# Transposes of 128 rows cut into two halves of 64 rows, a whole group per PSUM tile, in an attention and expert kernel

## The chip, the cores and the metric

The kernel runs on one core of one Trainium2 chip. The metric is the device time of one execution in microseconds. Three runs of the kernel before took 462.81, 463.68 and 463.78 us, the median is 463.68 us.

## The reference

Attention over 8 batches, 12 heads, 448 positions and a head size of 64, with q and k normalised row by row, is followed by a layer of 8 experts, of which each token takes one and each expert keeps 80 tokens at most. Tokens that no expert keeps give rows of zeros.

```python
q_n, k_n = rmsnorm(q, g_q), rmsnorm(k, g_k)          # x / sqrt(mean(x*x) + 1e-6) * g
attn = softmax(q_n @ k_n.transpose(0, 1, 3, 2) / sqrt(64))
x = (attn @ v).transpose(0, 2, 1, 3).reshape(3584, 768)
logits = x @ w_gate                                   # 3584 x 8
expert_idx, gate_w = argmax(logits), softmax(logits)[expert_idx]
for e in range(8):
    tok = the tokens of e, those 80 with the largest gate_w where there are more
    out[tok] = gate_w[tok] * (relu(x[tok] @ w1[e]) @ w2[e])   # 768 -> 1024 -> 768
```

## The kernel before

Four heads of one batch make a group; there are 24 groups, 3 to a batch. A row tile `qk` holds, on its 128 partitions, two heads `u` of 64 positions each, and along the free axis 14 blocks: 7 position classes `x` for each of two further heads `hh`. Every group goes through these steps: ScalarE squares q and k (line 253), VectorE sums (261), ScalarE and VectorE form the inverse root (`rstd`, 272 to 276), VectorE multiplies (`qn`, 289), TensorE turns q and k (`transp`, 301) and ScalarE copies the turned rows out of PSUM into `qkT` (314 with the gain, 316 without). Then come 7 steps `score` and `av`: four pairs of 64x64 matmuls make scores of 64 keys for 448 queries of four heads (326), ScalarE takes the exponential of 128x896 (329), and the product with v is added up in `po` over the 7 steps (341). The program has float32 score and product matmuls as two instructions each in the profile, so a step is 8 instructions on line 326 and 8 on line 341. VectorE adds the exponentials up over the steps (`presum`, 357 and 359), for the softmax's denominator. After step 7 ScalarE copies `po` to `us` (348), and `xout` turns `us` back to rows (606), copies them to `xb` (611) and sends them to a scratch array in DRAM with three DMAs of the SP queue (619, 620).

Per batch, `zl` (376) makes the gate's sums and the denominators of the 3 groups in one tile, by 48 matmuls of 64x32; `gate1` copies its two halves out (381, 385) and adds them on VectorE (388); `gate1t` turns the result (393); `gate1v`, `gate2`, ... and the pieces of `merge` (line 482 on, PSUM tiles named `mp`) pick each token's expert and keep the list of the best 80 per expert. After the last batch the lists are finished and the experts' products run (905, 924), while weights come in and rows are scattered by DMA.

The order is written out by hand. The main loop goes over slots of two steps. A slot's order is: `begin` work, the scores of two steps, `presum` of the two steps before, `mid` work, the products `av` of those two steps, `end` work. `at_slot` puts a piece of work into a slot and one of these places. On every engine instructions run in this order. PSUM is divided so: `tp_ps` has two buffers of one bank (512 float32), for the turned tiles `tp`, `xp`, `zt`; `sc_ps` has two buffers of two banks, for the scores `ps`, the gate's sums `zl` and the scratch `mp` of `merge`; `po_ps` has one buffer of two banks. An instruction that writes a buffer waits until the last reader of its former content is done.

In `transp(g, a, f)` the 7 turns of a tensor are cut into `f` = 0 with 4 and `f` = 1 with 3, each with a PSUM tile and a copy of its own, each in a slot of its own; in `xout(g, u)` the two halves `u` have 4 turns, a PSUM tile, a copy and a slot each. Each turn is one instruction:

```python
nc.tensor.transpose(tp[:, x * 128:(x + 1) * 128], qn[...128 rows x 128 columns...], ident[:, :])
```

It loads 128x128 float32 as weights and streams the identity of 128 columns past them.

Of the kernel before, what the change touches and what calls it, by code (L numbers as in the profile page):

```python
# [10 lines left out]
F32 = mybir.dt.float32  # L11
BF16 = mybir.dt.bfloat16
AF = mybir.ActivationFunctionType
# [4 lines left out]
PSUM = bass.MemoryType.PSUM  # L18
# [3 lines left out]
def kernel(  # L22
# [13 lines left out]
    nc = tc.nc  # L36

    B, H, S, D = q.shape
# [9 lines left out]
    NX = S // 64  # L48
# [4 lines left out]
    NJ = SM // 128  # L53
    NQ = H // 4
    NG = B * NQ
# [17 lines left out]
    ident = cpool.tile([128, 128], F32, name="ident")  # L73
# [15 lines left out]
    def gains():  # L89

        t = gk[0]
        grow = t[:1, 256:384]
        nc.vector.tensor_mul(grow, t[:1, 0:128], t[:1, 128:256])
        nc.vector.tensor_scalar_mul(grow, grow, 1.0 / math.sqrt(D))
        gp = tpps.tile([128, 512], F32, tag="tp", name="gp")
        nc.tensor.matmul(gp[:, 0:1], grow, one[:, :], start=True, stop=True)
        nc.vector.tensor_copy(gqk[:, :], gp[:, 0:1])

# [100 lines left out]
        load_weights(wpool, e, e)  # L199

    gpool = ctx.enter_context(tc.tile_pool(name="gate", bufs=2))
    tpps = ctx.enter_context(tc.tile_pool(name="tp_ps", bufs=2, space=PSUM))
    ctx.enter_context(tc.manual_schedule())

    ps_stack = ExitStack()
# [10 lines left out]
    with av_stack:  # L216
# [75 lines left out]
                    rs[:, lo:hi].rearrange("p (hh x) -> p hh x", x=NX)  # L292
                    .unsqueeze(3).to_broadcast([128, h1 - h0, NX, D]))

        def transp(g, a, f):

            tp = tpps.tile([128, 512], F32, tag="tp", name="tp")
            qn = st[g]["qn%d" % a]
            x0, n = (0, 4) if f == 0 else (4, NX - 4)
            for x in range(n):  # L300
                nc.tensor.transpose(  # L301
                    tp[:, x * 128:(x + 1) * 128],
                    qn[:, 2 * (x0 + x):2 * (x0 + x) + 2].rearrange("p h d -> p (h d)"),
                    ident[:, :])
            if f == 0:
                st[g]["T%d" % a] = qktpool.tile([128, 2, S], F32, tag=f"qkT{a}", name="qkT")
            o = st[g]["T%d" % a][:, :, x0 * 64:(x0 + n) * 64].rearrange(
                "q u (x p) -> q x u p", p=64)
            i = tp[:, :n * 128].rearrange("q (x u p) -> q x u p", u=2, p=64)

            if g == 0 and a and f == 0:
                nc.vector.tensor_scalar_mul(o, i, gqk[:, :])
            elif a == (g == 0):
                nc.scalar.activation(o, i, AF.Copy, scale=gqk[:, :])  # L314
            else:
                nc.scalar.copy(o, i)  # L316

        def score(r):
            g, x = divmod(r, RD)
# [41 lines left out]
        def zl(b, groups):  # L361


            if groups[0] == 0:
                gst[b]["zl"] = scps.tile([128, 2, 512], F32, tag="sc", name="zl")
            t = gst[b]["zl"]
            for i in groups:
                s = st[NQ * b + i]
                for c in range(4):
                    for r in range(2):  # L370
                        p = slice(64 * r, 64 * r + 64)
                        if c // 2 == r:
# [15 lines left out]
                nc.vector.tensor_add(zsb[:, c], zsb[:, c], other[:, c])  # L388

        def gate1t(b):  # L390
            zt = tpps.tile([128, 512], F32, tag="tp", name="zt")
# [204 lines left out]
            return [[row, lambda: vbeat((0, 1))], [experts, lambda: vbeat((2, 3)), vtied],  # L596
                    [own, vahead], [counts, vput], [place], [turn]]

        def xout(g, u):

            b, i = divmod(g, NQ)
            xp = tpps.tile([128, 512], F32, tag="tp", name="xp")
            us = st[g]["us"]
            for j in range(NJ + 1):
                c = j * 128 if j < NJ else S - 128
                nc.tensor.transpose(xp[:, j * 128:(j + 1) * 128], us[:, u, c:c + 128],  # L606
                                    ident[:, :])
            if u == 0:
                st[g]["xb"] = prep.tile([128, NJ + 1, 256], F32, tag="xb", name="xb")
            xb = st[g]["xb"]  # L610
            nc.scalar.copy(xb[:, :, u * 128:(u + 1) * 128],  # L611
                           xp[:, :].rearrange("p (j d) -> p j d", d=128))
            if u == 0:
                return
# [26 lines left out]
        def at_slot(where, s, f, *a):  # L641
            where.setdefault(s, []).append((f, a))
# [5 lines left out]
        lo, hi = HALF  # L648
        for f, *a in ((square, 0, lo), (square, 0, hi), (squares, 0, lo), (root, 0, lo),
                      (square, 1, lo), (squares, 0, hi), (root, 0, hi), (square, 1, hi),  # L650
                      (inverse, 0, lo), (normalise, 0, lo), (inverse, 0, hi),
                      (normalise, 0, hi), (squares, 1, lo), (root, 1, lo), (squares, 1, hi),
                      (root, 1, hi), (transp, 0, 0), (transp, 0, 1), (inverse, 1, lo),
                      (normalise, 1, lo), (inverse, 1, hi), (normalise, 1, hi), (gains, ),
                      (exptable, ), (transp, 1, 0)):
            at_slot(mid, -10, f, *([0] if a else []), *a)
        for g in range(NG):
            b0 = g * RD // 2
            odd = g % 2
            at_slot(begins, max(b0 - 11, -10), load_qk, g)  # L660
            at_slot(begins, b0 - 4, load_v, g)
            if g:
                for a in range(2):
                    at_slot(mid, b0 - 7 + a if g > 1 else -1, square, g, a)
                    at_slot(end, b0 - 7 + a if g > 1 else -1, squares, g, a)
                at_slot(mid, b0 - 5 if g > 1 else 0, rstd, g)
                for a in range(2):
                    at_slot(mid, b0 - 5 + a if g > 1 else 0, normalise, g, a)
            for a in range(2):
                for f in range(2):  # L670
                    t = b0 - 4 + 2 * a + f
                    if g == 0 and a + f < 2 or g == 0 and a > f:
                        continue
                    if g < 2:
                        t += 2 if g == 1 and a + f == 0 else 1
                    at_slot(end, t, transp, g, a, f)
            at_slot(end, b0 + 4 + odd, xout, g, 0)
            at_slot(end, b0 + 5 + odd, xout, g, 1)
        for b in range(B):
            b0 = (NQ * b + NQ - 1) * RD // 2  # L680
            if b == B - 1:
                at_slot(end, b0 + 3, zl, b, range(NQ - 1))
                at_slot(end, b0 + 4, zl, b, range(NQ - 1, NQ))
                at_slot(end, b0 + 4, gate1, b)
                at_slot(end, b0 + 5, gate1t, b)
# [67 lines left out]
    hot = tpps.tile([128, 512], F32, tag="tp", name="hot")  # L753

    def busy(n):

# [220 lines left out]
```

## Time and profile before

| | |
|---|---|
| median of 3 runs | 463.68 us (462.81 to 463.78) |
| profiled execution, its own time | 463.21 us |
| its span, first to last instruction | 461.3 us |
| TensorE busy | 440.2 us (95%) |
| VectorE busy | 358.3 us (78%) |
| ScalarE busy | 327.6 us (71%) |
| mean granted TensorE clock | 0.982 |

Between the span and the execution's own time lie 1.9 us. A share of busy time is a mean over the whole span; the attention part goes up to about 394 us, the experts' part takes the rest. PE stands for TensorE's matmuls, PEld for its weight loads, DVE for VectorE, ACT for ScalarE. A group of pipelined matmuls that overlap counts its time once.

### The profile page before, as it was taken

The numbers are of one execution on the slowest core, as the hardware profiler recorded it, in microseconds if no ns is written. First come the engines' busy times: TensorE is split into PE (matmuls) and PEld (weight loads), VectorE is DVE, ScalarE is ACT, GpSimd is POOL, SyncE is SP. The second block draws the span as 40 slices with busy tenths as digits, with TensorE's granted clock in tenths as the row PEclk, the third lists the DMA queues.
The fourth block names the chain that finished last, engine by engine and source line by source line (L and its number), as shares of the span: only waits on it lengthen the run. The fifth ranks groups of instructions, "written<-read, shape, count | busy, mean of one in ns | idle before, by whom it ended". The sixth has DMA issues, their size and how long they took to land.

```text
span 461.3 us, 11332 instructions
## 1 busy us (share of the span) xinstructions
PE 440.2 (95%) x4639; PEld 215.7 (47%) x4639; DVE 358.3 (78%) x650; ACT 327.6 (71%) x537; POOL 64.6 (14%) x126
## 2 busy tenths in 40 slices
PE   6999999999999999999999999999999999789894
PEld 5344444453444434443444444534444344348673
DVE  5788759995999878987998699959996877454451
ACT  6788878887888868986988699778887766301111
POOL 4010000200040004000510030001200010362311
PEclk9799999999999999999999999999999999979998
DMA  8999565898489966992799949956996376749991
GB/s 235 261 245 322 175 191 157 148 255 296 144 159 253 304 179 129 239 339 58 184 234 249 349 104 216 299 176 197 180 263 201 93 155 268 278 111 335 365 351 44
DMA packets 67530, 100.83 MB, mean 219 GB/s; under 512 B 7880, under 2 KB 59176, under 8 KB 66200
## 3 DMA queue, kind: packets, MB, share of 16 engines
q1 hardware_dynamic: 51184, 70.05, 47.0%
q0 software_dynamic: 16000, 29.61, 33.5%
q8 instruction: 36, 0.59, 0.5%
q10 hardware_dynamic: 296, 0.46, 0.3%
q14 instruction: 14, 0.11, 0.1%
HBM read 101.11 MB, written 39.89 MB: 306 GB/s over the span
## 4 chain that ended last, share of the span: by engine, by line
PE 84%; issue 7%; DVE 3%; ACT 3%; POOL 2%; DMA 1%; POOLq 0%
PE ps L326 30%; PE po L341 28%; PE tp L301 9%; PE xp L606 6%; PE zl L376 5%; POOL out_dram L937 2%; PE hot L758 1%; PE zt L393 1%; PE mp L496 1%; ACT zo L385 1%; DMA qk<-in_q_dram 1%; PE py L924 1%; POOL xg L868 1%; ACT zsb L381 1%; PE mp L550 1%
## 5 line engine op out<-in xcount | busy, mean ns | idle before, releaser
L329 ACT ACTIVATE at<-ps 128x896 f32<-128x896 f32 x168 | 146.4, 923 | 16.9 <-PE ps L326 15.0
L326 PE MATMUL ps<-qkT 64*64 64x448 f32 x1344 | 149.9, 557 | 2.3 <-ACT zo L385 1.5
L341 PE MATMUL po<-at,vt 64*64 64x448 f32 x1344 | 144.2, 538 | 0.0
L359 DVE TENSOR_TENSOR sm<-sm,at 128x896 f32<-128x896 f32 x120 | 131.0, 1091 | 3.3
L341 PEld LDWEIGHTS po<-at,vt 64*64 64x64 f32 x1344 | 50.0, 133 | 71.9 <-issue 66.6
L326 PEld LDWEIGHTS ps<-qkT 64*64 64x64 f32 x1344 | 43.3, 134 | 66.1 <-issue 40.0
L261 DVE TENSOR_REDUCE ms<-sq 128x14 f32<-128x896 f32 (+1 forms) x50 | 52.0, 1046 | 23.6 <-ACT sq L253 23.2
L289 DVE TENSOR_TENSOR qn<-qk,rs 128x896 f32<-128x896 f32 (+1 forms) x50 | 52.5, 1051 | 1.3
L301 PE MATMUL tp<-ident,qn 128*128 128x128 f32 x336 | 52.7, 281 | 0.4 <-DVE qn L289 0.4
L253 ACT ACTIVATE sq<-qk 128x896 f32<-128x896 f32 (+1 forms) x50 | 46.2, 927 | 2.4 <-DMA qk<-in_q_dram 2.0
L301 PEld LDWEIGHTS tp<-ident,qn 128*128 128x128 f32 x336 | 37.4, 142 | 15.2 <-ACT at L329 7.1
L476 POOL CAST pt<-gw 128x4 bf16<-128x4 f32 x8 | 1.6, 197 | 304.9 <-DVE gw L451 304.9
L611 ACT COPY xb<-xp 128x512 f32<-128x512 f32 x48 | 28.4, 591 | 13.6 <-PE xp L606 13.5
L909 ACT ACTIVATE h_sb<-ph 128x320 bf16<-128x320 f32 x16 | 6.9, 438 | 43.8 <-PE ph L905 36.8
L606 PEld LDWEIGHTS xp<-ident,us 128*128 128x128 f32 x192 | 20.5, 141 | 24.9 <-issue 18.4
L314 ACT ACTIVATE qkT<-tp,gqk 128x384 f32<-128x384 f32 (+1 forms) x47 | 30.2, 644 | 1.9 <-PE tp L301 1.9
L606 PE MATMUL xp<-ident,us 128*128 128x128 f32 x192 | 31.1, 284 | 0.0
L316 ACT COPY qkT<-tp 128x512 f32<-128x512 f32 (+1 forms) x48 | 25.7, 537 | 7.0 <-PE tp L301 6.1
L924 PE MATMUL py<-w_sb,h_sb 128*80 128x384 bf16 x128 | 23.5, 328 | 2.9 <-issue 2.0
L348 ACT COPY us<-po 128x896 f32<-128x896 f32 (+1 forms) x24 | 21.4, 891 | 6.8 <-PE po L341 6.7
L357 DVE TENSOR_TENSOR sm<-at 128x896 f32<-128x896 f32 x24 | 26.0, 1082 | 0.0
L376 PE MATMUL zl<-us,wgs 64*32 64x448 f32 x192 | 20.8, 541 | 0.7 <-ACT us L348 0.7
(171 smaller groups left out, 404.0 us busy)
## 6 DMA issues: line engine op xcount, KB each, us to landing
wb_scratch<-in_moe_w_dram POOLq DMA_DIRECT2D x20, 768.0 KB, 16.1
w_sb<-wb_scratch SPq DMA_DIRECT2D x10, 1536.0 KB, 21.9
vt<-in_v_dram SPq DMA_DIRECT2D x24, 448.0 KB, 7.1
out_dram<-zeros SPq DMA_DIRECT2D x28, 384.0 KB, 4.6
qk<-in_q_dram SPq DMA_DIRECT2D x23, 448.0 KB, 7.4
qk<-in_k_dram SPq DMA_DIRECT2D x23, 448.0 KB, 7.2
w_sb<-in_moe_w_dram POOLq DMA_DIRECT2D x6, 1536.0 KB, 24.1
xr_scratch<-xb SPq DMA_DIRECT2D x46, 192.0 KB, 7.4
```

The source lines that it names most:

```text
L253: nc.scalar.activation(st[g]["sq%d" % a][:, lo:hi], st[g]["qk"][a][:, lo:hi], AF.Square)
L261: nc.vector.reduce_sum(out=st[g]["ms"][:, a, lo:hi], in_=st[g]["sq%d" % a][:, lo:hi], axis=AX.X)
L289: nc.vector.tensor_mul(qn[:].rearrange("p (x hh) d -> p hh x d", hh=2)[:, h0:h1], qk[:, lo:hi].rearrange("p (hh x) d -> p hh x d", x=NX), ...
L301: nc.tensor.transpose(tp[:, x * 128:(x + 1) * 128], qn[:, 2 * (x0 + x):2 * (x0 + x) + 2].rearrange("p h d -> p (h d)"), ident[:, :])
L314: nc.scalar.activation(o, i, AF.Copy, scale=gqk[:, :])
L326: nc.tensor.matmul(ps[u * 64:u * 64 + 64, hh, :S], T1[d, u, x * 64:(x + 1) * 64], T0[d, u, :], start=True, stop=True)
L329: nc.scalar.activation(at[:], ps[:, :, :S], AF.Exp)
L341: nc.tensor.matmul(po[hh * D:(hh + 1) * D, u, :S], vt[p, hh * NX + x, :], at[p, hh, :], start=(x == 0), stop=(x == RD - 1))
L359: nc.vector.tensor_add(s["sm"][:], s["sm"][:], s["at%d" % x][:])
L376: nc.tensor.matmul(t[32 * c:32 * c + 32, r, :S], w, x, start=(i == 0), stop=(i == NQ - 1))
L606: nc.tensor.transpose(xp[:, j * 128:(j + 1) * 128], us[:, u, c:c + 128], ident[:, :])
L611: nc.scalar.copy(xb[:, :, u * 128:(u + 1) * 128], xp[:, :].rearrange("p (j d) -> p j d", d=128))
```

## The change

Every turn of q, k and `us` is cut in two. A new helper `turned` turns 64 rows of 128 columns: the weights are 64 partitions by 128 columns, the identity that streams past has 64 columns, and the tile position says that the instruction uses rows 0 to 63 or rows 64 to 127 of the array. The two halves of a turn follow each other and write to different banks of one PSUM tile of two banks. `transp` now turns all 7 blocks of a tensor at once, 14 halves, with one copy of 128x896 behind them; in the first group k's copy is split between VectorE and ScalarE. `xout` turns both `u` at once, 16 halves, with one copy of 128x1024. The pool `tp_ps` has one buffer of two banks in place of two of one. The gate's sums `zl` take that buffer, but for the last batch, and no longer one of the scores' buffers; `zl` and `gate1` stand in `mid` in place of `end`, so before the slot's products. The slots of `transp` and `xout` are written anew.

```diff
-    tpps = ctx.enter_context(tc.tile_pool(name="tp_ps", bufs=2, space=PSUM))
+    tpps = ctx.enter_context(tc.tile_pool(name="tp_ps", bufs=1, space=PSUM))
...
+        def turned(o, w, p):
+            nc.tensor.transpose(o, w, ident[p, p], tile_position=(p.start, 0))
+
-        def transp(g, a, f):
-
-            tp = tpps.tile([128, 512], F32, tag="tp", name="tp")
+        def transp(g, a):
+
+            if g or not a:
+                tp = tpps.tile([128, 2, 512], F32, tag="tp", name="tp")
+            else:
+                tp = scps.tile([128, 2, 512], F32, tag="sc", name="tp")
             qn = st[g]["qn%d" % a]
-            x0, n = (0, 4) if f == 0 else (4, NX - 4)
-            for x in range(n):
-                nc.tensor.transpose(
-                    tp[:, x * 128:(x + 1) * 128],
-                    qn[:, 2 * (x0 + x):2 * (x0 + x) + 2].rearrange("p h d -> p (h d)"),
-                    ident[:, :])
...
+            for x in range(NX):
+                for u in range(2):
+                    p = slice(64 * u, 64 * u + 64)
+                    turned(tp[:, u, x * 64:(x + 1) * 64],
+                           qn[p, 2 * x:2 * x + 2, :].rearrange("p h d -> p (h d)"), p)
+            if g == 0 and a:
+                c = 4 * 64
+                nc.vector.tensor_scalar_mul(T[:, :, :c], tp[:, :, :c], gqk[:, :])
+                nc.scalar.activation(T[:, :, c:], tp[:, :, c:S], AF.Copy, scale=gqk[:, :])
             elif a == (g == 0):
-                nc.scalar.activation(o, i, AF.Copy, scale=gqk[:, :])
+                nc.scalar.activation(T[:], tp[:, :, :S], AF.Copy, scale=gqk[:, :])
             else:
-                nc.scalar.copy(o, i)
+                nc.scalar.copy(T[:], tp[:, :, :S])
...
-                gst[b]["zl"] = scps.tile([128, 2, 512], F32, tag="sc", name="zl")
+                pool, tag = (tpps, "tp") if b < B - 1 else (scps, "sc")
+                gst[b]["zl"] = pool.tile([128, 2, 512], F32, tag=tag, name="zl")
...
-        def xout(g, u):
+        def xout(g):
...
             for j in range(NJ + 1):
-                c = j * 128 if j < NJ else S - 128
-                nc.tensor.transpose(xp[:, j * 128:(j + 1) * 128], us[:, u, c:c + 128],
-                                    ident[:, :])
...
+                for u in range(2):
+                    c = slice((2 * j + u) * 64, (2 * j + u) * 64 + 64)
+                    for hh in range(2):
+                        p = slice(64 * hh, 64 * hh + 64)
+                        t = min(j * 128, S - 128)
+                        turned(xp[:, hh, c], us[p, u, t:t + 128], p)
+            xb = prep.tile([128, NJ + 1, 256], F32, tag="xb", name="xb")
+            nc.scalar.copy(xb[:].rearrange("p j (u hh d) -> p hh (j u) d", u=2, hh=2),
+                           xp[:].rearrange("p hh (k d) -> p hh k d", d=D))
...
-                    at_slot(end, t, transp, g, a, f)
-            at_slot(end, b0 + 4 + odd, xout, g, 0)
-            at_slot(end, b0 + 5 + odd, xout, g, 1)
+                    at_slot(end, b0 - (3 if g > 1 else 2) + a, transp, g, a)
+            last = g % NQ == NQ - 1 and g < NG - 1
+            if g < NG - 1:
+                at_slot(end, b0 + 6 + last * (1 if odd else 4), xout, g)
...
-            at_slot(end, b0 + 5, zl, b, range(NQ))
-            at_slot(end, b0 + 5, gate1, b)
+            at_slot(mid, b0 + 5, zl, b, range(NQ))
+            at_slot(mid, b0 + 5, gate1, b)
```

The first place is TensorE behind the gate's sums of a batch (`ps` scores, `po` products, `tp` turns of q or k, `zt` turn of the gate's sums). Before, from the last of the 48 matmuls of `zl` on:

```order
L376 MATMUL zl<-us,wgs 32x448
L326 MATMUL ps<-qkT 64x448 x8
L341 MATMUL po<-at,vt 64x448 x8
L301 MATMUL tp<-ident,qn 128x128 x7
L393 MATMUL zt<-ident,zsb 128x128 x4
L326 MATMUL ps<-qkT 64x448 x8
```

and now, from the turns before `zl` on, with the 46 middle matmuls of `zl` left out:

```order
L296 MATMUL tp<-ident,qn 128x64 x14
L329 MATMUL ps<-qkT 64x448 x8
L380 MATMUL zl<-us,wgs 32x448
...
L380 MATMUL zl<-us,wgs 32x448
L344 MATMUL po<-at,vt 64x448 x8
L296 MATMUL tp<-ident,qn 128x64 x14
L329 MATMUL ps<-qkT 64x448 x8
L344 MATMUL po<-at,vt 64x448 x8
L397 MATMUL zt<-ident,zsb 128x128 x4
```

`zl` stood between a slot's turns and the next slot's scores; it stands now between the scores and the products of one slot, and the next turns, which take the same PSUM buffer, come after the products. The turn `zt` has a slot of its own.

The second place is TensorE two slots later in the same batch, where the first piece of `merge` (`mp`, 128x128) stands beside the turns (`xp`). Before:

```order
L341 MATMUL po<-at,vt 64x448 x8
L496 MATMUL mp<-ident,gw 128x128 x4
L606 MATMUL xp<-ident,us 128x128 x4
L301 MATMUL tp<-ident,qn 128x128 x3
L326 MATMUL ps<-qkT 64x448 x8
```

and now:

```order
L344 MATMUL po<-at,vt 64x448 x8
L500 MATMUL mp<-ident,gw 128x128 x4
L296 MATMUL xp<-ident,us 128x64 x16
L329 MATMUL ps<-qkT 64x448 x8
```

A visit that was 128x128 throughout now has a 128x128 part and a 64x128 part.

## Rows read from the trace of the kernel before

**Rows 1.** Windows: us, then PE, PEld, DVE, ACT, POOL busy, clock, DMA share, GB/s.

```profile
111.54:161.99 50.45, 49.89 (x525) 22.90 (x524) 43.87 (x78) 41.58 (x70) 5.00 (x10) 1.00 0.82 207
...
390.70:461.30 70.60, 57.44 (x715) 38.54 (x714) 31.74 (x87) 11.17 (x25) 23.60 (x31) 0.93 0.69 243
```

**Rows 2.** Groups by form: operation, shape, count | busy us, mean ns | idle before, releaser.

```profile
L326 PE MATMUL ps<-qkT 64*64 64x448 f32 x1344 | 149.9, 557 | 2.3 <-ACT zo L385 1.5 <-DVE qkT L312 0.8
L301 PE MATMUL tp<-ident,qn 128*128 128x128 f32 x336 | 52.7, 281 | 0.4 <-DVE qn L289 0.4
L606 PE MATMUL xp<-ident,us 128*128 128x128 f32 x192 | 31.1, 284 | 0.0
```

**Rows 3.** Timeline of PE: start, length, line, tile, count [idle before].

```profile
103.55 1.73 PE L326 MATMUL ps<-qkT 64*64 64x448 f32 x16
105.11 1.68 PE L341 MATMUL po<-at,vt 64*64 64x448 f32 x16
106.72 0.21 PE L592 MATMUL mp<-identb,listn 80*24 80x80 bf16 x1
...
122.66 0.65 PE L301 MATMUL tp<-ident,qn 128*128 128x128 f32 x4
123.24 0.98 PE L341 MATMUL po<-at,vt 64*64 64x448 f32 x8
...
168.01 0.98 PE L301 MATMUL tp<-ident,qn 128*128 128x128 f32 x7
```

**Rows 4.** Timeline of PEld: first load of a turn, first two, four of the scores.

```profile
168.01 0.14 PEld L301 LDWEIGHTS tp<-ident,qn 128*128 128x128 f32 x1 [0.71 <-issue]
168.01 0.20 PEld L301 LDWEIGHTS tp<-ident,qn 128*128 128x128 f32 x2 [0.71 <-issue]
...
170.14 0.15 PEld L326 LDWEIGHTS ps<-qkT 64*64 64x64 f32 x4 [0.22 <-issue]
```

**Rows 5.** Source L726, 5 to 7 us: loads, min/median/max ns, first and last start.

```profile
L726 PEld LDWEIGHTS wps<-zeros x13: 190/190/191, 4.9 to 6.8; 128*128 128x128 f32 x13
```

**Rows 6.** Timeline of PE: four matmuls of 8 columns; group of their line.

```profile
144.05 0.24 PE L550 MATMUL mp<-eqb,beat 128*128 128x8 bf16 x4
...
L550 PE MATMUL mp<-eqb,beat 128*128 128x8 bf16 x112 | 4.4, 166 | 0.0
```

**Rows 7.** Timeline of PE behind the gate's sums of one batch.

```profile
113.96 0.98 PE L326 MATMUL ps<-qkT 64*64 64x448 f32 x8
115.15 0.98 PE L326 MATMUL ps<-qkT 64*64 64x448 f32 x8 [0.21 <-ACT zo L385]
...
118.90 0.66 PE L393 MATMUL zt<-ident,zsb 128*128 128x128 f32 x4 [0.35 <-ACT xb L611]
```

**Rows 8.** Groups by form on ACT: the copies out of PSUM.

```profile
L611 ACT COPY xb<-xp 128x512 f32<-128x512 f32 x48 | 28.4, 591 | 13.6 <-PE xp L606 13.5
L348 ACT COPY us<-po 128x896 f32<-128x896 f32 x23 | 20.9, 907 | 3.7 <-PE po L341 3.6
L314 ACT ACTIVATE qkT<-tp,gqk 128x512 f32<-128x512 f32 x23 | 15.8, 687 | 1.9 <-PE tp L301 1.9
L314 ACT ACTIVATE qkT<-tp,gqk 128x384 f32<-128x384 f32 x24 | 14.5, 604 | 0.0
L316 ACT COPY qkT<-tp 128x512 f32<-128x512 f32 x24 | 14.2, 591 | 1.3 <-PE tp L301 0.4
L316 ACT COPY qkT<-tp 128x384 f32<-128x384 f32 x24 | 11.6, 482 | 5.7 <-PE tp L301 5.7
L381 ACT COPY zsb<-zl 128x448 f32<-128x448 f32 x8 | 4.3, 532 | 14.7 <-PE zl L376 14.7
```

**Rows 9.** Groups by form on DVE with the longest idle time before them.

```profile
L261 DVE TENSOR_REDUCE ms<-sq 128x14 f32<-128x896 f32 x46 | 49.7, 1083 | 20.3 <-ACT sq L253 19.9
L388 DVE TENSOR_TENSOR zsb<-zsb,zo 128x448 f32<-128x448 f32 x7 | 4.4, 625 | 19.2 <-ACT zo L385 19.2
```

**Rows 10.** DMA issues: KB each, median us from issue to landing.

```profile
qk<-in_q_dram SPq DMA_DIRECT2D x23, 448.0 KB, 7.4
```

More of the change, by code (lines that the diff above doesn't have):

```diff
@@ L94, in gains @@
         nc.vector.tensor_scalar_mul(grow, grow, 1.0 / math.sqrt(D))
-        gp = tpps.tile([128, 512], F32, tag="tp", name="gp")
-        nc.tensor.matmul(gp[:, 0:1], grow, one[:, :], start=True, stop=True)
-        nc.vector.tensor_copy(gqk[:, :], gp[:, 0:1])
+        gp = scps.tile([128, 2, 512], F32, tag="sc", name="gp")
+        nc.tensor.matmul(gp[:, 0, 0:1], grow, one[:, :], start=True, stop=True)
+        nc.vector.tensor_copy(gqk[:, :], gp[:, 0, 0:1])
     assert NQ * E == 24
@@ L293, in normalise @@
                     .unsqueeze(3).to_broadcast([128, h1 - h0, NX, D]))
-        def transp(g, a, f):
-            tp = tpps.tile([128, 512], F32, tag="tp", name="tp")
-            qn = st[g]["qn%d" % a]
-            x0, n = (0, 4) if f == 0 else (4, NX - 4)
-            for x in range(n):
-                nc.tensor.transpose(
-                    tp[:, x * 128:(x + 1) * 128],
-                    qn[:, 2 * (x0 + x):2 * (x0 + x) + 2].rearrange("p h d -> p (h d)"),
-                    ident[:, :])
[L305 to L312, printed above, removed]
+        def turned(o, w, p):
[5 more added lines that the diff above has]
+                tp = scps.tile([128, 2, 512], F32, tag="sc", name="tp")
+            qn = st[g]["qn%d" % a]
+            T = qktpool.tile([128, 2, S], F32, tag=f"qkT{a}", name="qkT")
+            st[g]["T%d" % a] = T
+            for x in range(NX):
[7 more added lines that the diff above has]
+                nc.scalar.activation(T[:, :, c:], tp[:, :, c:S], AF.Copy, scale=gqk[:, :])
             elif a == (g == 0):
-                nc.scalar.activation(o, i, AF.Copy, scale=gqk[:, :])
+                nc.scalar.activation(T[:], tp[:, :, :S], AF.Copy, scale=gqk[:, :])
             else:
-                nc.scalar.copy(o, i)
+                nc.scalar.copy(T[:], tp[:, :, :S])
         def score(r):
@@ L390, in gate1t @@
         def gate1t(b):
-            zt = tpps.tile([128, 512], F32, tag="tp", name="zt")
+            zt = tpps.tile([128, 2, 512], F32, tag="tp", name="zt")[:, 0, :]
             for j in range(NJ + 1):
@@ L597, in merge @@
                     [own, vahead], [counts, vput], [place], [turn]]
-        def xout(g, u):
+        def xout(g):
             b, i = divmod(g, NQ)
-            xp = tpps.tile([128, 512], F32, tag="tp", name="xp")
+            pool, tag = (tpps, "tp") if g < NG - 1 else (scps, "sc")
+            xp = pool.tile([128, 2, 512], F32, tag=tag, name="xp")
             us = st[g]["us"]
             for j in range(NJ + 1):
-                c = j * 128 if j < NJ else S - 128
-                nc.tensor.transpose(xp[:, j * 128:(j + 1) * 128], us[:, u, c:c + 128],
-                                    ident[:, :])
[L608 to L614, printed above, removed]
+                for u in range(2):
[7 more added lines that the diff above has]
+                           xp[:].rearrange("p hh (k d) -> p hh k d", d=D))
             rows = xr_dram[b * S:(b + 1) * S, i * 256:(i + 1) * 256].rearrange(
@@ L652 @@
                       (normalise, 0, hi), (squares, 1, lo), (root, 1, lo), (squares, 1, hi),
-                      (root, 1, hi), (transp, 0, 0), (transp, 0, 1), (inverse, 1, lo),
+                      (root, 1, hi), (transp, 0), (inverse, 1, lo),
                       (normalise, 1, lo), (inverse, 1, hi), (normalise, 1, hi), (gains, ),
-                      (exptable, ), (transp, 1, 0)):
+                      (exptable, ), (transp, 1)):
             at_slot(mid, -10, f, *([0] if a else []), *a)
@@ L668 @@
                     at_slot(mid, b0 - 5 + a if g > 1 else 0, normalise, g, a)
[L669 to L675, printed above, removed]
-                    at_slot(end, t, transp, g, a, f)
-            at_slot(end, b0 + 4 + odd, xout, g, 0)
-            at_slot(end, b0 + 5 + odd, xout, g, 1)
+            if g:
+                for a in range(2):
+                    at_slot(end, b0 - (3 if g > 1 else 2) + a, transp, g, a)
+            last = g % NQ == NQ - 1 and g < NG - 1
+            if g < NG - 1:
+                at_slot(end, b0 + 6 + last * (1 if odd else 4), xout, g)
         for b in range(B):
@@ L684 @@
                 at_slot(end, b0 + 4, gate1, b)
+                at_slot(end, b0 + 4, xout, NG - 1)
                 at_slot(end, b0 + 5, gate1t, b)
@@ L751 @@
     mpool = ctx.enter_context(tc.tile_pool(name="moe_sb", bufs=2))
-    hot = tpps.tile([128, 512], F32, tag="tp", name="hot")
+    hot = tpps.tile([128, 2, 512], F32, tag="tp", name="hot")[:, 0, :]
     def busy(n):
```

## The prediction

> **What bounds the kernel now.** I read the busy time by windows first, one window for a batch, from one start of the gate's sums to the next. The reader is to see that a batch takes 50.45 us and that TensorE is busy for 49.9 us of it, at a granted clock of 1.00, while VectorE has 43.9 us (87%) and ScalarE 41.6 us (82%) [rows 1]. Eight batches like this one make up the attention part. Then I read the costliest groups: TensorE's score group sat idle for 2.3 us in the whole run, the turns for 0.4 us and 0.0 us [rows 2]. So in the attention part what leaves TensorE's stream shortens the run, one for one, until VectorE or ScalarE is full. The window from 390.70 us on is the last batch's gate and the experts, which the change hardly touches; it keeps its 70.6 us [rows 1].
>
> **Cost of a turn now.** In the timeline four turns take 0.65 us and seven take 0.98 us [rows 3], so one more turn costs (0.98 - 0.65)/3 = 0.11 us; I use 0.109, within the rounding. Streaming 128 identity columns is then 0.85 ns a column. The weight load is not what sets this: one load is 0.14 us long, and two together 0.20 us, so the second began 0.06 us behind the first, while the first turn was still streaming [rows 4]. A load thus occupies its path for 0.06 us and hides behind 0.109 us of streaming.
>
> There are 336 turns on line 301 and 192 on line 606 [rows 2]: 528 x 0.109 = 57.6 us of TensorE.
>
> **Cost of a turn after.** It becomes two halves on rows 0 to 63 and 64 to 127. Each streams 64 columns, 64 x 0.85 = 0.054 us, and each still loads 128 columns of weights, 0.06 us if the load of 64 partitions goes as that of 128. No 64x128 tile is in this trace, so I bound the pair. If the halves run side by side, a pair costs the larger of the two, 0.06 us. What speaks for side by side: 16 score instructions take 1.73 us where one alone has a mean of 557 ns [rows 2, 3]. At 0.85 ns a column 448 columns are 0.38 us, and 16 of them one after the other would be 6.1 us. Four run at a time, and two of these four differ only in the row half, with their outputs in two banks, just as the new halves have them. Their four loads are done in 0.15 us together [rows 4]. The lower bound is the spacing of the smallest load-and-matmul pairs: four matmuls of 8 columns take 0.24 us, one alone 0.166 us, so (0.24 - 0.166)/3 = 0.025 us each and 0.05 us for two [rows 6]. The upper bound is halves one after the other, 2 x 0.06 = 0.12 us. I take 0.06, since the score instructions are the nearest rows.
>
> A second reading of the load: the float32 loads of `wps`, also 128 columns, are 190 ns long at full clock [rows 5] and not 140. They belong to plain matmuls and not to turns, so I let the halves keep the turns' shorter load; if they had the longer one, 0.05 us more occupy the path, a pair costs 0.11 us and nothing is won.
>
> The Trainium skill, "TensorE: Matmul & The Clock Gate", "Part 3: Packing small matmuls — row/col tiling", says that a weight load overlaps with running matmuls only where the row groups differ. By that rule a turn of 128 rows would cost load plus stream today, 0.06 + 0.109 = 0.17 us, and a pair of halves later 0.06 + 0.054 = 0.114 us per row half, so the sum would be won from another start and no time would be left to win against 0.109. The trace does not agree: the second load of a turn begins on the same rows 0.06 us in, and the turns follow at 0.109 us [rows 3, 4].
>
> The sum of this part: 528 x (0.109 - 0.06) = 25.9 us less TensorE. The ends are 528 x 0.059 = 31.2 us less and 528 x 0.011 = 5.8 us more.
>
> **Switches of the array's shape.** Four turns take 0.58 us up to the next group where 4 x 0.109 = 0.44 us is streaming: 0.14 us are lost on leaving. Sixteen products take 1.50 us of streaming (16/4 x 0.375) and 1.61 us up to the next group of another shape: 0.11 us on entering [rows 3]. So an edge costs some 0.13 us. I counted edges in the order over two batches: 48 before, 57 after. Fewer visits are not the point, since each slot has about one either way; what is new is that a 128x128 piece of `merge` beside 64x128 turns makes an edge inside a visit, and that `zl` has one of its own. Nine more in two batches, 31 in seven batches: 31 x 0.13 = 4.1 us more. From below 0 (if 128x128 beside 64x128 is no new shape to the array), from above twice that, 8 us.
>
> The Trainium skill, "TensorEngine Tiling (Array Packing)", "Key Properties", says that changing the tiling mode drains the engine. The 0.11 and 0.14 us show it here, so by the rule the 4.1 us stand, and by the reading that only column tiling counts they would be 0.
>
> **The gate's sums out of the scores' ring.** Today the second score step behind `zl` starts 1.19 us after the first instead of 0.75, because it waits for the copy `zo`, and `zt` waits 0.35 us for a copy of `xb` [rows 7]: 0.8 us a batch, 5.5 us in seven. Both go. What is late next: the turns behind the products now need `zl`'s buffer, which is free after the two copies of 0.53 us each [rows 8]. Counted from the start of `zl`: its 48 matmuls take 2.4 us (111.54 to 113.96 [rows 1, 7]), the copies end at some 3.7, the semaphore makes it 3.9, and the products let TensorE reach the turns at 2.4 + 1.5 = 3.9 us. They just meet; behind the waiting turns stand the next scores, so any lag of ScalarE there is paid in full. I book 0.2 us a batch, so 4 us less, with ends of 0 and 5.5.
>
> **One buffer for turned tiles.** A burst of turns must find the copy of the last burst done. Bursts are a slot apart, some 4.5 us, the copy is about 1 us. ScalarE itself gets less: a group's six copies are 0.69 + 0.60 + 0.59 + 0.48 + 2 x 0.59 = 3.55 us, and become one of 896 columns at 0.91 (as line 348), one with the gain at about 1.0 and one of 1024 at about 1.03 (both estimated by the rows' slope of 0.85 ns a column), 2.94 us [rows 8]. That is 0.6 us a group or 14.6 us of ScalarE, all off the path while TensorE is full. In the slots where `xb`'s copy of 1.03 us now stands ahead of `us`'s, the products of the next group come some 0.4 us later. `xout`'s three SP DMAs move with it, up to four slots later, and loads of q, k and v that stood behind them on SP go ahead; with 7.4 us from issue to landing of such a load [rows 10] and loads issued several slots early I cost this at nothing. If that cover failed, ScalarE's squares would wait.
>
> **VectorE.** The period goes from 50.45 to about 50.45 - 66 x 0.049 + 0.6 - 0.6 = 47.2 us (66 turns a batch), and VectorE's 43.9 us are then 93% of it. Its order is fixed, and it stands idle for 20.3 us behind squares and 19.2 us behind `zo` in the run [rows 9]. There are six buffers of exponentials, so it may lag by two slots before TensorE notices. I book 3 us for that and the later `us` together, from 0 to 8.
>
> **Sum.** -25.9 + 4.1 - 4 + 3 = -22.8 us on 463.2 us of the profiled execution gives 440.4. The median of the runs is 0.5 us above that execution, so I forecast 441 us. First group and last batch are in the 528 and get no term of their own.
>
> **Rivals.**
> - The halves do not run side by side. Loads of the two row halves share one path and follow each other at 0.06 us, so a pair costs 0.12: +5.8 + 4.1 - 4 + 0, some 469 us. The place is every burst; it decides against the kernel as soon as a pair costs more than 0.109 us. Against it: the four loads of the scores within 0.15 us [rows 4]; for it: no load of 128 columns on half the rows is in the trace, and a weight path could be full with 128 columns.
> - The load of a half goes at the slow rate of [rows 5]: a pair costs 0.11, the turns win nothing, and edges and ring cancel: 463 us, no change. For it: the tile is new to the engine; against it: the operation is the same as in the turns of today.
> - VectorE becomes the bound. If it keeps its idle time behind `zo` (19.2/7 = 2.7 us a batch) and behind the squares (20.3/8 = 2.5 us), a batch needs 43.9 + 5.2 = 49.1 us and seven batches give 7 x 1.4 = 10 us: 453 us. Against it: both waits are for ScalarE, which is paced by TensorE and comes earlier with it.
> - Better than thought: a pair at the floor of 0.05 us, no price for edges: -31 - 4 + 1, 430 us.
>
> **Chances.** The forecast (434 to 447 us) 0.62; VectorE as bound (447 to 458) 0.13; no gain from the load (459 to 465) 0.09; one after the other (465 to 473) 0.09; better than 434 us 0.07. From 432 to 461 us the range holds the first two, half of the last and a third of the third, some 0.8. A measurement of this kernel can't tell less than 0.2%, 0.9 us, from no change. Faster by more: 0.62 + 0.13 + 0.07 and less than half of the third, 0.85; the same 0.05; slower 0.10.
>
> **What would show it.** In the profile of the changed kernel: 14 halves of q or k in about 7 x 0.06 + 0.22 = 0.64 us against 0.98 for seven turns; at 0.98 or more the side-by-side run is wrong. The period between two `zl` near 47.2 us. No wait for `zo` before scores, and one of at most a few tenths before the turns behind `zl`. VectorE near 93% in a batch's window; if TensorE shows idle time behind `at` copies or `qn`, VectorE or ScalarE is the bound. The experts' part at 70 us as now. The forecast is wrong if a pair of halves costs 0.1 us or more, or if TensorE's idle time in a batch grows above 2 us.

## The result, and the profile after

Four runs of the changed kernel took 438.43 to 442.68 us, median 440.09 us; the kernel before took 463.73 us beside them. The ratio is 0.9485 (95% interval 0.9421 to 0.9549). The forecast was 441 us. The profiled execution is the slowest of the four: 442.68 us, span 440.8 us.

The first view is that of the windows, over the same two batches of both kernels, from one start of the gate's sums to the next but one (us, then PE, PEld, DVE, ACT, POOL busy, clock, DMA share, GB/s). Two batches are needed because the single ones alternate. Before, the shorter of the two batches alone (the longer is in [rows 1]), then both:

```profile
65.64:111.54 45.90, 45.55 (x484) 20.91 (x483) 39.58 (x68) 38.03 (x62) 3.70 (x9) 1.00 0.85 213
...
65.64:161.99 96.35, 95.44 (x1008) 43.81 (x1007) 83.45 (x145) 79.61 (x131) 8.70 (x19) 1.00 0.83 210
```

After, two batches and then each of them:

```profile
105.98:196.19 90.21, 89.49 (x1142) 39.59 (x1138) 82.96 (x145) 76.30 (x113) 9.68 (x21) 1.00 0.90 232
...
105.98:152.70 46.72, 46.41 (x590) 20.32 (x586) 42.14 (x73) 39.72 (x59) 4.97 (x10) 1.00 0.92 235
152.70:196.19 43.49, 43.09 (x557) 19.27 (x553) 40.82 (x73) 36.57 (x55) 4.70 (x11) 1.00 0.89 228
```

Two batches cost 6.14 us less, and TensorE's busy time fell by 5.95 us of it. The whole profiled execution became 20.5 us shorter: the first gate's sums begin at 62.47 us in place of 65.64, the six batches from there to the seventh gate's sums take 270.91 us in place of 289.05, the stretch from these to the last gate's sums takes 37.05 us in place of 35.99, and the rest 70.4 us in place of 70.6. Those six batches are the steady part: the two further traces of the changed kernel (c_after, c_after2) have 270.87 and 270.88 us for them, while the start lies between 58.7 and 62.5 us and the rest between 70.4 and 72.8. VectorE's busy time stayed and is now 92% of the time (94% in the shorter batch); ScalarE's fell by 3.3 us and has 85%. The clock is at its full level in both.

The second view is the groups by form. The turns of the changed kernel, and the copies behind them, answer to [rows 2, 8] (PE's shapes there are the array's tile, rows by columns, then what streams past):

```profile
L296 PE MATMUL tp<-ident,qn 64*128 64x64 f32 x672 | 31.2, 230 | 1.0 <-ACT qkT L317 1.0
L617 ACT COPY xb<-xp 128x1024 f32<-128x1024 f32 x24 | 24.3, 1012 | 9.6 <-PE xp L296 8.9
L317 ACT ACTIVATE qkT<-tp,gqk 128x896 f32<-128x896 f32 x23 | 23.5, 1021 | 0.0
L319 ACT COPY qkT<-tp 128x896 f32<-128x896 f32 x24 | 22.0, 917 | 10.0 <-PE tp L296 10.0
L296 PE MATMUL xp<-ident,us 64*128 64x64 f32 x384 | 17.1, 229 | 0.0
```

The two groups of turns were busy for 83.8 us before and are now for 48.3 us. That is a sum over bursts with their tails; what a burst costs the stream is read from starts. The third view is the timeline of PE in the changed kernel (start, length, line, tile, count), answering to [rows 3, 7]:

```profile
108.39 1.73 PE L344 MATMUL po<-at,vt 64*64 64x448 f32 x16
110.06 0.65 PE L296 MATMUL tp<-ident,qn 64*128 64x64 f32 x14
110.64 1.74 PE L329 MATMUL ps<-qkT 64*64 64x448 f32 x16
...
125.62 0.65 PE L500 MATMUL mp<-ident,gw 128*128 128x128 f32 x4
126.20 0.65 PE L296 MATMUL tp<-ident,qn 64*128 64x64 f32 x14
126.78 1.74 PE L329 MATMUL ps<-qkT 64*64 64x448 f32 x16
...
130.27 0.71 PE L296 MATMUL xp<-ident,us 64*128 64x64 f32 x16
130.91 1.74 PE L329 MATMUL ps<-qkT 64*64 64x448 f32 x16
```

14 halves take 0.58 us up to the next group, 16 take 0.64 us: a pair more costs 0.06 us. In the trace's single records the pairs start 0.062 us apart from the second on; I use 0.0625. Taken off, 0.58 - 7 x 0.0625 leaves 0.14 us for the edge, the change of the array's shape. The four whole turns of `mp` ahead of them need 4 x 0.109 = 0.44 us and take 0.58, so there is an edge between 128x128 and 64x128 as well; what it costs is read against whole turns below. The turns at 110.06 are the ones behind `zl`; they start 1.67 us after the products in front of them, which is the 1.61 us of an undisturbed pass and 0.06 us more.

### The profile page after: what moved, and what is told of

Its sections match the earlier page's. It is cut to its first block, busy times and chain, and to the rows that moved or that the text cites. A ratio compares the mean times of both kernels' runs of the same rounds, so it can differ in the third digit from the quotient of the medians.

```text
span 440.8 us, 12293 instructions
## 1 busy us (share of the span) xinstructions
PE 417.5 (95%) x5167; PEld 199.4 (45%) x5167; DVE 357.2 (81%) x650; ACT 314.9 (71%) x466; POOL 64.9 (15%) x126
## 4 chain that ended last, share of the span: by engine, by line
PE 44%; DVE 26%; ACT 10%; issue 9%; DMA 6%; POOL 3%; POOLq 0%; DVEq 0%; ACTq 0%; SPq 0%
PE ps L329 16%; PE po L344 15%; DVE sm L362 7%; PE zl L380 5%; DVE qn L289 4%; ACT at L332 4%; DVE ms L261 4%; PE tp L296 3%; DMA qk<-in_k_dram 3%; PE xp L296 2%; ACT sq L253 2%; DMA xr_scratch<-rz 2%; POOL out_dram L938 2%; DVE beat L510 2%; DVE sm L360 1%
## 5 line engine op out<-in xcount | busy, mean ns | idle before, releaser
L296 PEld LDWEIGHTS tp<-ident,qn 64*128 64x128 f32 x672 | 24.6, 139 | 26.3 <-ACT at L332 10.6
L296 PE MATMUL tp<-ident,qn 64*128 64x64 f32 x672 | 31.2, 230 | 1.0 <-ACT qkT L317 1.0
L617 ACT COPY xb<-xp 128x1024 f32<-128x1024 f32 x24 | 24.3, 1012 | 9.6 <-PE xp L296 8.9
L319 ACT COPY qkT<-tp 128x896 f32<-128x896 f32 x24 | 22.0, 917 | 10.0 <-PE tp L296 10.0
L317 ACT ACTIVATE qkT<-tp,gqk 128x896 f32<-128x896 f32 x23 | 23.5, 1021 | 0.0
L380 PE MATMUL zl<-sm,zsel 64*32 64x448 f32 x192 | 20.6, 540 | 0.0
L930 DVE TENSOR_SCALAR yo<-py,gwT 80x384 f32<-80x384 f32 (+1 forms) x16 | 9.6, 600 | 12.3 <-PE py L925 12.3
```

What stands on the lines that cost most here:

```text
L296: nc.tensor.transpose(o, w, ident[p, p], tile_position=(p.start, 0))
L317: nc.scalar.activation(T[:], tp[:, :, :S], AF.Copy, scale=gqk[:, :])
L380: nc.tensor.matmul(t[32 * c:32 * c + 32, r, :S], w, x, start=(i == 0), stop=(i == NQ - 1))
L617: nc.scalar.copy(xb[:].rearrange("p j (u hh d) -> p hh (j u) d", u=2, hh=2), xp[:].rearrange("p hh (k d) -> p hh k d", d=D))
```

## The experiments

All times are medians. The kernels were run in sets; those of one set share a chip and the runs of the kernel before, and kernels of different sets are compared by their ratio to it. "Two batches" is read from each trace as above.

| kernel | us | ratio to before (95%) | two batches, us |
|---|---|---|---|
| before | 463.7 to 464.6, 462.5 in the set of e_ring, e_ramp, e_dve and e_more | 1 | 96.35 |
| changed (c_after) | 441.72 | 0.9511 (0.9484 to 0.9539) | 90.20 |
| changed (c_after2) | 441.08 | 0.9503 (0.948 to 0.9525) | 90.21 |
| e_serial | 455.65 | 0.9803 (0.9772 to 0.9833) | 93.52 |
| e_whole | 458.46 | 0.9864 (0.9847 to 0.9881) | 94.43 |
| e_halves | 505.21 | 1.0881 (1.0863 to 1.09) | 106.0 |
| e_ring | 446.77 | 0.9645 (0.9612 to 0.9677) | 91.72 |
| e_ramp | 439.74 | 0.9505 (0.948 to 0.9529) | 90.23 |
| e_dve | 439.90 | 0.949 (0.9462 to 0.9518) | 89.77 |
| e_more | 439.38 | 0.9497 (0.947 to 0.9523) | 90.00 |
| e_pool | 440.15 | 0.9469 (0.9449 to 0.9489) | 90.11 |
| e_best | 440.01 | 0.9471 (0.9449 to 0.9494) | 90.13 |

**The changed kernel again.** 

> The changed kernel once more, for comparison on this chip: 438 to 443 us.

 Measured 441.72 us.

**Whole turns in the new frame (e_whole).** One tile of two banks, one copy and the new slots stay; each turn is one 128x128 instruction again.

```diff
-            for x in range(NX):
-                for u in range(2):
-                    p = slice(64 * u, 64 * u + 64)
-                    turned(tp[:, u, x * 64:(x + 1) * 64],
-                           qn[p, 2 * x:2 * x + 2, :].rearrange("p h d -> p (h d)"), p)
+            tf = tp[:].rearrange("q b c -> q (b c)")
+            for x in range(NX):
+                nc.tensor.transpose(tf[:, x * 128:(x + 1) * 128],
+                                    qn[:, 2 * x:2 * x + 2, :].rearrange("p h d -> p (h d)"),
+                                    ident[:, :])
...
```

> The changed kernel with whole 128x128 turns in place of halves; one tile of two banks, one copy, the new slots and zl's place stay. Side by side: the 24.5 us of the turns come back and some 4 us of shape edges beside merge go, 459 to 465 us. Rival (one tile, one copy and the new slots make the gain): 438 to 446 us.

Measured 458.46 us, 16.7 us above the changed kernel on the same chip and a hair under the lower end of what side-by-side halves were to give. The window of e_whole:

```profile
107.61:202.04 94.43, 94.43 (x1010) 44.22 (x1006) 83.41 (x144) 76.83 (x113) 9.92 (x21) 1.00 0.86 221
```

TensorE is busy for all 94.43 us; with halves it is busy for 4.94 us less, and the two batches are 4.22 us shorter. Both kernels have the same groups of TensorE work in these two batches, in the same order, so the starts can be set side by side, group by group. The first piece of `merge` and the turns behind it, in e_whole:

```profile
127.80 0.65 PE L501 MATMUL mp<-ident,gw 128*128 128x128 f32 x4
128.29 0.93 PE L309 MATMUL tp<-ident,qn 128*128 128x128 f32 x7
129.15 0.61 PE L330 MATMUL ps<-qkT 64*64 64x448 f32 x4
```

Here `mp` takes 0.49 us up to the turns, where it takes 0.58 us beside halves. Read so, the 18 bursts of turns lose 6.29 us by halves (0.33 us where there are seven pairs, 0.38 where there are eight). Six places where a piece of `merge` on the whole array (128x128, twice 80x80) now stands beside 64x128 turns cost 0.74 us, 0.10 to 0.15 us each. And 1.35 us are stops that e_whole does not have, of which the profile shows 0.72 as idle time: the length of a matmul's record covers the first part of a wait behind it. The longest stop, in the changed kernel and then the same place in e_whole:

```profile
188.87 0.33 PE L586 MATMUL mp<-info,put 128*80 128x40 bf16 x4
189.60 0.48 PE L590 MATMUL mp<-listn,keep 80*80 80x5 bf16 x8 [0.40 <-DVE keep L578]
```

```profile
194.67 0.33 PE L587 MATMUL mp<-info,put 128*80 128x40 bf16 x4
194.84 0.46 PE L591 MATMUL mp<-listn,keep 80*80 80x5 bf16 x8
```

From start to start these are 0.73 and 0.17 us. So 6.29 - 0.74 - 1.35 = 4.2 us arrive. The rest of the change, e_whole against before, is worth 1.92 us in two batches, and 6.1 us in all. The rival, that the frame (the merged tile, its one copy, the new slots) makes the gain, falls: it makes about a quarter.

**The same halves, not in pairs (e_serial).** All halves of rows 0 to 63 first, then those of rows 64 to 127; `xout` likewise.

```diff
-            for x in range(NX):
-                for u in range(2):
+            for u in range(2):
+                for x in range(NX):
                     p = slice(64 * u, 64 * u + 64)
...
```

> The changed kernel with the same halves in another order: first all those on rows 0 to 63, then all those on rows 64 to 127. Side by side (my theory): pairs that now cost 0.0625 us can no longer overlap, since neighbours share a row half, and each half costs about 0.062 us by its weight load, so 528 x 0.062 = 33 us more TensorE, 470 to 475 us. Rival (the gain comes from fewer columns per instruction, not from two row halves at once): the order does not matter, 438 to 443 us.

Measured 455.65 us, 13.9 us more. The order alone decides, so the rival of fewer columns is out; but I expected more than twice that. The window of two batches, and the timeline of PE:

```profile
107.25:200.77 93.52, 93.52 (x1142) 44.45 (x1138) 83.21 (x145) 76.70 (x113) 9.92 (x21) 1.00 0.88 222
...
136.42 0.89 PE L296 MATMUL tp<-ident,qn 64*128 64x64 f32 x14
137.23 0.61 PE L329 MATMUL ps<-qkT 64*64 64x448 f32 x4
```

14 halves take 0.81 us up to the next group. Less the 0.14 us of the edge that is 0.67 us, or 11 steps of 0.061 us: not 14, as one after the other would need, and not 7. The halves of the second row group begin before the first row group is through, so that three pairs still overlap. The single records of this burst bear it out: the 14 halves begin at 11 places in time, three of which hold two halves each, 4 to 7 ns apart, while the others follow each other at 55 to 63 ns (the first two at 111). Writing the halves alternately lets all seven overlap.

**Halves in the old frame (e_halves).** The kernel before with each turn as two halves into a tile of two banks, of which PSUM holds one.

```diff
-    tpps = ctx.enter_context(tc.tile_pool(name="tp_ps", bufs=2, space=PSUM))
+    tpps = ctx.enter_context(tc.tile_pool(name="tp_ps", bufs=1, space=PSUM))
...
-                nc.tensor.transpose(xp[:, j * 128:(j + 1) * 128], us[:, u, c:c + 128],
-                                    ident[:, :])
+                for hh in range(2):
+                    p = slice(64 * hh, 64 * hh + 64)
+                    turned(xp[:, hh, j * 64:(j + 1) * 64], us[p, u, c:c + 128], p)
...
```

> The kernel before with halves alone: a tile of two banks and one buffer for turns, as PSUM has no more room, but tensors still cut in f = 0 and 1 and u = 0 and 1, each with its copy, zl in the scores' buffers and the old slots. Some 44 visits have xp and tp behind each other; with one buffer the second waits for ScalarE's copy of the first, about 1 us. My theory: -24 from the halves, +25 to +50 from these waits, 465 to 490 us. Rival (halves alone carry the gain): 438 to 444 us.

Measured 505.21 us, slower than before by 40.6 us and beyond the end of what I expected. The waits of PE (who, for whom, us in total, times, longest):

```profile
PE tp L296 <- ACT xb L615: 34.7, 38, 1.4
PE tp L296 <- ACT qkT L319: 8.6, 13, 1.3
```

and one of them in its timeline:

```profile
121.99 0.46 PE L296 MATMUL xp<-ident,us 64*128 64x64 f32 x8
123.13 0.47 PE L296 MATMUL tp<-ident,qn 64*128 64x64 f32 x8 [0.68 <-ACT xb L615]
```

The idle time is 43 us on these two lines, and the stop is longer than the idle time shows (1.14 us from burst to burst for four pairs, 0.25 us of streaming). So halves in two banks need the rest of the change: with one copy per burst and no two bursts in a slot, one buffer is enough without such a wait. What the merged tile saves by itself no run shows apart from the other parts of the frame.

**The gate's sums back in the scores' ring (e_ring).**

```diff
-                pool, tag = (tpps, "tp") if b < B - 1 else (scps, "sc")
+                pool, tag = scps, "sc"
```

> The changed kernel with the gate's sums of every batch back in the scores' two buffers; their new slot stays, everything else too. If leaving the ring matters: the scores of the next slot wait for the copy zo, 0.4 us a batch as before or more, since zl now stands behind the slot's scores and takes the buffer that the second score step still needs: +3 to +12 us, 444 to 454 us. Rival (the ring is free there): as the changed kernel, 440 to 443 us.

Measured 446.77 us; by the ratios 1.4% slower, some 6 us, inside the range. The timeline shows a wait that the changed kernel has not, at the first matmul of `zl`:

```profile
105.22 0.56 PE L380 MATMUL zl<-us,wgs 64*32 64x448 f32 x1 [0.64 <-ACT at L332]
```

It comes back seven times, and two batches take 1.51 us more. In the new slot, behind the scores, `zl` needs a buffer that the exponential still reads.

**Does VectorE bound it (e_dve).** The comparison of ties is left out in the first 7 batches.

```diff
-            return [[row, lambda: vbeat((0, 1))], [experts, lambda: vbeat((2, 3)), vtied],
+            return [[row, lambda: vbeat((0, 1))], [experts, lambda: vbeat((2, 3))],
...
```

> The changed kernel without the comparison of ties (vtied, 28 operations of 347 ns) in the first 7 batches; that part of the result is left out. If VectorE is now the bound, as the rival of the prediction has it: up to 9.7 us less, 432 to 438 us. If TensorE still is: within 1 us of the changed kernel.

Measured 439.90 us, a ratio that can't be told from the changed kernel's. In the window VectorE had 1.84 us less to do in two batches and these became 0.44 us shorter:

```profile
104.98:194.75 89.77, 89.29 (x1143) 39.51 (x1139) 81.12 (x137) 76.31 (x113) 9.69 (x21) 1.00 0.90 232
```

So VectorE is not the bound, but it is last in some places: TensorE's wait for `keep`, 0.4 us in the changed kernel's two batches, is 0.2 us here. Over the six steady batches e_dve is 1.5 us shorter (269.40 against 270.88 us).

**More turns as halves (e_more).** `zt` and the first piece of `merge`, each in the first 7 batches.

```diff
-                    nc.tensor.transpose(ps[:, 0, j * 128:j * 128 + 128],
-                                        m["gw"][:, j:j + 1].to_broadcast([128, 128]),
-                                        ident[:, :])
+                    for r in range(2):
+                        p = slice(64 * r, 64 * r + 64)
+                        turned(ps[:, r, j * 64:j * 64 + 64],
+                               m["gw"][p, j:j + 1].to_broadcast([64, 128]), p)
...
```

> The changed kernel with two more turns as halves of 64 rows in the first 7 batches: zt (four turns a batch) and the first piece of merge (four turns a batch). Halves save 8 x 0.047 us a batch, and the piece of merge beside turns of 64x128 loses its shape edge of about 0.145 us: 7 x 0.52 = 3.6 us less, 437 to 439 us. Rival (an edge costs nothing): 2.6 us less.

Measured 439.38 us: no difference to be told in the whole, and 0.6 us less in the six steady batches (270.28 against 270.88 us). Here the time was saved and given back. The timeline of PE shows the saving:

```profile
121.84 0.45 PE L296 MATMUL mp<-ident,gw 64*128 64x64 f32 x8
122.12 0.60 PE L296 MATMUL tp<-ident,qn 64*128 64x64 f32 x14
```

`mp` takes 0.28 us up to the turns where it took 0.58: the halves are shorter and the edge is gone, and TensorE's busy time in the window fell by 0.89 us:

```profile
102.21:192.21 90.00, 88.60 (x1158) 38.93 (x1154) 82.99 (x145) 76.15 (x113) 9.67 (x21) 1.00 0.91 231
```

But the window is only 0.21 us shorter. PE's waits in it, against the changed kernel's in its two batches:

```profile
PE mp L599 <- DVE keep L587: 0.6, 2, 0.4
PE ps L329 <- ACT at L332: 0.4, 1, 0.4
PE mp L595 <- DVE put L583: 0.3, 1, 0.3
```

```profile
PE mp L590 <- DVE keep L578: 0.4, 1, 0.4
PE ps L329 <- ACT at L332: 0.2, 1, 0.2
```

Most of what TensorE no longer does it now waits, for VectorE's pieces of the gate and for the exponentials.

**That work off VectorE (e_pool), and the first loads (e_ramp, e_best).** e_pool is e_more with the ties on GpSimd; e_ramp is the changed kernel, and e_best is e_pool, with the work of group 2 one slot later.

```diff
-                    nc.vector.scalar_tensor_tensor(
-                        tied[:, j], row[:, j * 128:(j + 1) * 128], gw[:, j:j + 1], tri[:, :],
-                        op0=ALU.is_equal, op1=ALU.mult)
+                    nc.gpsimd.tensor_scalar(tied[:, j], row[:, j * 128:(j + 1) * 128],
+                                            gw[:, j:j + 1], None, op0=ALU.is_equal)
...
+                late = g == 2
-                    at_slot(mid, b0 - 7 + a if g > 1 else -1, square, g, a)
+                    at_slot(mid, b0 - 7 + late + a if g > 1 else -1, square, g, a)
...
```

> The kernel with zt and the first piece of merge as halves, and the comparison of ties moved from VectorE to GpSimd (six operations a batch in place of four). In the run with the two more turns as halves alone, two batches took 90.05 us against 90.22, where 1.04 us less was expected, and TensorE waited for VectorE's keep. If VectorE's place before keep took the rest: two batches 88.8 to 89.3 us, and 4 to 5 us less than the changed kernel in all. Rival (halves of these turns save nothing by themselves): 89.8 us as in the run without the ties, 1 to 2 us less.

> The changed kernel with the squares, sums, roots and products of group 2 alone one slot later, so that ScalarE does not stop in front of the loads of q and k of that group. The trace of the changed kernel has 2.5 us of TensorE idle between 20 and 28 us behind it. If the first loads set that stretch: -1.5 to -3 us, 438.5 to 440.5 us. Rival (VectorE or the exponentials set it): no change, or slower by a new wait before the turns of group 2.

> The same and the work of group 2 one slot later. If the late loads of the first groups can be hidden so: the first gate's sums start at about 58 us instead of 61 to 62 us, 1.5 to 3 us less than the run without it. Rival (the start varies by itself as much): no difference that can be told.

> The changed kernel once more beside these two: 438 to 443 us, two batches 90.2 us.

e_pool took 440.15 us and e_best 440.01, against 441.08 for the changed kernel on the same chip; the intervals of the ratios (up to 0.9489 and 0.9494, from 0.948) touch, so a gain of the whole, 0.2% by the medians and 0.35% by the ratios, is not shown. Nor did the later slot move the start: the first gate's sums began at 58.6 us in e_best and at 58.8 in e_pool, so the rival holds there. Two batches of e_pool took 90.11 us, so the expected 88.8 to 89.3 failed, and its six steady batches took 270.26 us, as long as those of e_more. VectorE was not relieved: it has eight operations fewer in the window, and its busy time is where it was.

```profile
101.81:191.92 90.11, 88.67 (x1159) 38.92 (x1155) 83.09 (x137) 76.20 (x113) 24.50 (x33) 1.00 0.89 225
```

The groups by form on VectorE, in the windows of e_pool and then of e_more, show why: its pieces of `beat` became longer. All 14 of them took 6.9 us in place of 4.9, and the 12 of `qn` 13.5 in place of 13.1.

```profile
L522 DVE TENSOR_SCALAR beat<-row,gw 128x64 bf16<-128x64 f32 x2 | 1.3, 650 | 0.0
L289 DVE TENSOR_TENSOR qn<-qk,rs 128x896 f32<-128x896 f32 x12 | 13.5, 1128 | 0.3
```

```profile
L522 DVE TENSOR_SCALAR beat<-row,gw 128x64 bf16<-128x64 f32 x2 | 0.5, 250 | 0.0
L289 DVE TENSOR_TENSOR qn<-qk,rs 128x896 f32<-128x896 f32 x12 | 13.1, 1088 | 0.3
L528 DVE SCALAR_TENSOR_TENSOR tied<-row,gw,tri 128x128 bf16<-128x128 f32 x8 | 2.3, 345 | 0.0
```

The pieces that grew most stand where GpSimd ends the product of the ties and goes on to its own DMA issues. First GpSimd over the whole run of e_pool, then GpSimd and VectorE at one such place (start, length):

```profile
L528 POOL TENSOR_SCALAR tied<-row,gw 128x128 bf16<-128x128 f32 x28 | 33.9, 1224 | 10.2 <-ACT row L512 10.2
...
127.41 2.78 POOL L531 TENSOR_TENSOR tied<-tied,tri 128x256 bf16<-128x256 bf16 x2
130.14 0.83 POOL L189 DMA_DIRECT2D wb_scratch<-in_moe_w_dram  x1
...
130.33 0.64 DVE L522 TENSOR_SCALAR beat<-row,gw 128x64 bf16<-128x64 f32 x1
```

Which of GpSimd's operations makes them longer is not shown. And this run neither refutes nor shows the rival that the halves of these turns save nothing by themselves: the relief of VectorE that was to be tested did not happen.

e_ramp's ratio is the changed kernel's. In its trace the first gate's sums began at 59.1 us, in the three of the changed kernel at 62.5, 61.4 and 58.7 us: the start varies by as much as was to be won. The waits that the slot was moved for, in the changed kernel's trace,

```profile
24.88 0.65 PE L296 MATMUL tp<-ident,qn 64*128 64x64 f32 x14 [0.97 <-ACT qkT L317]
...
27.76 1.03 PE L329 MATMUL ps<-qkT 64*64 64x448 f32 x4 [1.08 <-ACT qkT L319]
```

are gone in e_ramp, and one of 1.3 us before `po`, for `us`, stands in their place.

## Why the prediction was right, point by point

- **What bounds it.** TensorE did: e_whole and e_serial show no idle TensorE at all in two batches, and what their turns cost more is in the time. It is not quite one for one: of the 5.55 us that halves take out of TensorE's stream in two batches (6.29 less 0.74 of edges) 4.2 arrive. I took the one batch that I showed for all; the batches alternate, 45.90 and 50.45 us. The long one came out at 46.72 us, near my 47.2, and the short one at 43.49; the two together took 90.21 us, where 96.35 - 6.5 = 89.9 would have followed.
- **The pair of halves.** 0.06 us forecast, 0.0625 us read. The concurrency was inferred from the scores; e_serial shows that it is the two row groups that make it, since the same instructions without their neighbours on the other row group cost 13.9 us more. The term is 528 x 0.0465 = 24.6 us instead of 25.9 (25.2 by the bursts of e_whole).
- **The longer load of [rows 5].** The halves kept the turns' short one: their loads are 0.134 to 0.144 us long in the profile, with a median of 0.139, where that of the whole turns is 0.140.
- **The edges.** 4.1 us forecast for nine more in two batches. The price was right, the number was not: e_whole against the changed kernel shows six places in two batches, which cost 0.74 us, 2.6 us in seven.
- **The ring and `zt`.** 4 us forecast. The whole of the frame, of which this is a part, was worth 6.1 us by e_whole. The 0.2 us a batch that I booked for ScalarE's lag did not come: I had the copies of `zl` end 3.7 us after its start and gave the semaphore 0.2 us, which no row showed; the second copy ended after 3.56 us, and the turns behind the products began after 4.08 us without a wait. What I had not seen is that the move into `mid` needs the new buffer: in the scores' ring the moved `zl` costs 6 us.
- **VectorE and the later `us`.** 3 us forecast. The stops cost 1.35 us in two batches, 4.7 us in seven, though the profile shows 0.72 and 2.5 us as idle; the stretch from 20 to 30 us holds 2.5 us of idle time in one trace of the changed kernel and 1.3 us in another. I had charged VectorE; its `keep` makes about half of the 1.35 us, and the other waits named are for exponentials and, at the start, for copies behind late loads.
- **The sum.** -22.8 us forecast, -23.6 us by the medians. The mechanism held, but that the sum is within 1 us is in part luck: the pairs brought about 1 us less than forecast and the stops cost some 2 us more, while the edges were 1.5 us cheaper and the frame 2 us better. The rival that VectorE takes most of the gain (453 us) did not come, but e_more shows it one step away: the next 0.89 us off TensorE brought 0.21 us.

## What to carry to other kernels

A float32 turn of 128 rows was worth cutting into two row halves here, where streaming set its pace (0.109 us) and the weight load took its path for less (0.06 us). The halves must be written alternately; they went into two banks, and one bank for both was not tried. Count what the new tile shape does beside others, and how many PSUM buffers it leaves: the same halves made this kernel 9% slower where one buffer had to serve two bursts in a slot. Once the bound engine is within a few per cent of the next one, look for what waits there before shortening it again.

## What the runs showed of the hardware that was not expected

TensorE takes up halves for the other row group ahead of the remaining ones for the first: 14 halves in two blocks of seven took 0.81 us, where strict order would take 14 x 0.061 + 0.14 = 0.99 us. A change between array shapes cost 0.11 to 0.14 us each way by the starts, and 0.10 to 0.15 us between the whole array and 64x128, by e_whole against the changed kernel. A stop of TensorE is longer than its idle time in the profile: 1.35 us of stops in two batches showed as 0.72 us. The comparison of ties, 128x128 with a scalar per partition, takes 1224 ns on GpSimd and 345 ns, with the product included, on VectorE; and with it on GpSimd a VectorE comparison of 128x64 took 650 ns instead of 250, so that the 2.3 us that VectorE gave away in two batches were gone again, 2.0 us of them in the pieces of `beat` and 0.5 us in `qn`, by the sums of their lengths.
